# Crossbar transposes, 32x32 output tiles and a re-planned step order in a four-layer attention kernel

## The chip, the cores and the metric

The kernel runs on one core of one Trainium2 chip. The metric is the device time of one execution in microseconds (us). A profiled execution also has a span, from its first to its last instruction, which is a little shorter than its device time. Engines: TensorE (PE; PEld is its weight load), VectorE (DVE), ScalarE (ACT), GpSimd (POOL) and SyncE (SP), which issues almost all DMA transfers here.

## The reference, cut to what matters

Four layers work on one activation x of 2048 rows and 512 features, in the order A, B, A, B with the same weights for both A and both B. Each layer normalises x, computes an attention in 32 heads of 16 features, multiplies by an output matrix and adds the result to x.

```python
def _A_ref(x, wqkv, w_phi, wo):          # linear attention with learned features
    q, k, v = ...                        # x @ wqkv, heads of 16
    pq = einsum("bhsd,hdf->bhsf", q, w_phi)
    pk = einsum("bhsd,hdf->bhsf", k, w_phi)
    phi_q = concatenate([softmax(pq), softmax(-pq)])
    phi_k = concatenate([softmax(pk), softmax(-pk)])
    kv = einsum("bhsf,bhsd->bhfd", phi_k, v)     # sums over all 2048 rows
    z  = einsum("bhsf->bhf", phi_k)
    num = einsum("bhqf,bhfd->bhqd", phi_q, kv)
    den = einsum("bhqf,bhf->bhq", phi_q, z)[..., None] + 1e-6
    return (num / den) @ wo

def _B_ref(x, wqkv, wo):                 # window of 8 keys, 2 rows apart, looking back
    logits = einsum("bhsd,bhswd->bhsw", q, kg) * scale   # masked where the window leaves the sequence
    return einsum("bhsw,bhswd->bhsd", softmax(logits), vg) @ wo

x = x + _A_ref(layernorm(x), A...); x = x + _B_ref(layernorm(x), B...)   # twice
```

## The kernel before, in words

The 2048 rows are cut into four blocks (b = 0 to 3) of 512 rows, and each block into four tiles (t) of 128 rows. L = 0, 1 counts the pairs of layers. All products take bf16 inputs. Weight matrices, x and masks stay in SBUF; working tiles come from numbered slots of four pools ("big", "med", "t2" and the eight PSUM banks "ps").

The work is written as steps. Each `s_...` method of the class adds steps to threads, one thread for each stage and engine. The string `_ORDER` then says, step by step, which thread runs next, and so fixes the order of the instructions on TensorE, VectorE, ScalarE and on SyncE's queue: each engine works through its own list in that order and waits where an input or a buffer is not ready. `_CHOICE` has one digit for each flexible step (`flex`): a copy out of PSUM runs on VectorE (1) or ScalarE (0); a residual addition runs as one VectorE instruction (0, line 434) or as one more matmul with the identity on TensorE and a ScalarE copy (1, lines 424 and 431). `_SLOTS` names the buffer that each working tile gets. The setup (constants, masks, the first loads) stands in front of the steps and is not in `_ORDER`.

The stages:

- Fold (`s_fold`): the query and key weights of layer A are multiplied by `w_phi` once. The weights are transposed on TensorE (line 278), copied out, and multiplied by the block-diagonal `PHI` (line 289).
- Normalisation (`s_norm`): `ap` writes the normalised block xn (line 347). `pt` transposes it on TensorE, 16 transposes of 128x128 for a block (line 361), and `pe` copies the PSUM banks into xnT, two copies of 1024 columns for a block. A second way, `tr`, one transposing DMA for the whole block on SyncE's queue, stands in the code; `_OPT["tr_dma"]` names the blocks that take it, and is empty.
- Layer A, keys and values (`s_a1`): projections of keys (line 482) and values (line 494), exponentials of plus and minus the keys (line 488), softmax sums over f by three halving additions and a last one (`t8`, `t4`, `t2`, `t1`, lines 514 to 526), reciprocals through logarithm and exponential (`rr`), one product that normalises the exponentials (`mul`, line 534), and the key-value sums (`kv`, line 543): eight matmuls for each tile t, for the two signs and four groups of 128 columns, with 128 columns of features as weights and 129 moving columns (128 of values, and one of ones for z). They add up over all four blocks in three PSUM banks.
- Layer A, queries (`s_a2`): projections in transposed form (line 572), exponentials (line 580), softmax sums by small matmuls (line 588).
- `s_akv`: VectorE masks the finished sums into `ZM` (line 615) and into `R` (line 622), eight blocks of 128x128 of which the diagonal heads are kept. This needs the sums of all four blocks, so it separates the key side of a layer A from what follows.
- Layer A, denominators (`s_a3`): small matmuls with `ZM` (line 643), reciprocals, and the scaling of the query features, by broadcast matmuls for some blocks (lines 669 and 675) and by a DMA through DRAM for others (`Prho`).
- Layer A, output (`s_a4`): for each of four groups of heads two matmuls with a 128x128 block of `R` as weights and 512 moving columns (line 720), a copy into oT, then the output matrix (line 421), the residual and the statistics of the next normalisation (`s_out`).
- Layer B (`s_b1`, `s_b2`, `s_b3`): projections (line 742), a replication of the values along partitions by 16 DMAs for each block (`Vg`, line 794), the products with the window on VectorE (lines 823 and 883), sums of them by 32-column matmuls (lines 830 and 890), then the output matrix as in layer A. Block b needs the last rows of block b - 1.

Behind the last step a flag chooses whether a slower general path repeats the work; it is not taken for these inputs.

Of the kernel before, what the change touches and what calls it, by code (L numbers as in the profile page):

```python
# [19 lines left out]
H = 32  # L20
# [17 lines left out]
_OPT = {"rho_dma": ((0, 2), (0, 3), (1, 2), (1, 3)), "tr_dma": ()}  # L38
# [7 lines left out]
0 8l 0 4 4 1f 1 n 4 0 0 n 0 5 4 o 2 4 6 6 p n 2 n q u 3 u n n t 8 8 8 8 9 15 15 s 16 7 15 w 8 15 8 8 8 9i 17 v  # L46
a a a r u u y u b u 10 18 19 12 8 a i i z i i d d i 1g 1g 1d 1d c j i 13 13 1e 1e 1e x 12 13 13 d d k e i i i
1e 1d 1e 1e 12 12 k 1h l k 1d d 13 13 1i 11 d d d 2a d f f f f g 13 13 1a k m 1a 1a 1a 1g 1e 1e 1l 1l h 1z 20
2b 20 2c 1r 1z 20 1z 1z 20 1b 1r 1t 1l 2d 1l 1g 20 1k 2d 1s 20 20 20 1a 27 27 27 1o 1p 1o 11 11 14 1p 1p 1p 1r
1j 22 23 2c 2d 1o 1m 1p 22 1u 24 1p 27 1o 1l 1p 1p 2c 2c 2d 1w 22 22 1w 28 27 26 2d 2d 2d 25 1w 1w 1q 2b 2a 2b  # L50
1r 2a 2a 2d 1x 1c 1c 1c 1c 1n 2c 1n 1n 1n 2d 1w 1y 1y 1y 1v 1y 21 29 29 29 29 2b 2j 2j 2j 2j 2j 2j 31 2b 2b 2b
2b 2a 2b 2k 42 2l 2m 2l 2e 2e 43 2k 2l 2f 2l 2f 2f 2e 2l 2l 44 2f 43 2f 11 2e 2f 2f 2f 2k 2l 2l 2g 2h 2h 2e 2l
2f 5j 42 2g 2h 2l 2n 2n 2o 5k 43 43 2h 43 43 2n 5l 5k 5m 2p 2n 2g 2r 42 2g 43 32 43 43 43 2q 2s 2t 2s 2v 2s 45
45 ah 2h 2h 2w 45 2h 2h 46 47 2u 2u 2u 48 2s 2x 2u 2y 45 49 2u 2g 71 4a 2y 2y 2y 5m 4a 2y 4b 2s 2s 5m 2z 5k 5m
5k 2s 2s 4a 4e 4a 30 38 38 4c 2h 72 73 5n 5n 5n 4d 4c 11 4c 5o 3a 5p 72 33 33 4f 39 3d 5q 5n 4c 35 38 5r 5s 3b
34 4g 4c 3k 3d 4g 5s 5s 3e 2i 2i 5t 4g 4g 4a 4a 33 5w 4a 4g 4a 4h 3d 4i 5u 36 74 3f 74 74 3k 72 5v 5s 5u 5u 5x
5u 5y 5u 5y 74 38 4u 3c 4z 4u 4w 4p 4q 4p 4p 4r 72 3g 4k 4l 4k 4m 4k 51 4n 4v 75 75 77 76 4u 4x 3d 3h 3j 75 3i
4j 4u 4p 4y 5y 5y 5s 4t 5s 11 52 5y 3k 4k 78 50 51 4s 4o 51 75 79 5s 5s 60 7a 4j 7b 50 7c 7a 7d 7c 33 37 52 51
7a 7a 52 7f 5z 50 50 52 53 53 11 7e 7c 7c 3k 67 67 52 62 3l 7g 67 7c 7g 7a 7g 7g 7g 53 51 69 7a 7h 97 54 54 7a
7a 7i 3l 3l 3l 3m 3m 6c 6d 6c 6e 7p 7p 7q 68 3k 3l 6a 55 54 7k 7k 56 55 62 3m 7l 62 65 64 3j 54 7m 63 55 58 55  # L60
59 3j 3j 6c 3k 7u 6c 61 6f 6g 61 6i 7u 7p 67 3n 3o 6h 7w 6b 3n 3n 3n 3o 3q 6j 7p 7v 7s 6j 3o 3o 3s 7z 57 5a 5a
5d 5a 5b 3r 5c 6i 5a 5f 3p 3t 3t 3u 5c 3v 7k 5e 5c 6j 5c 5g 62 66 6j 5c 5g 3w 3v 3t 3t 3y 6k 6k 7r 6k 6k 6l 6l
5a 5g 5g 5a 6i 7u 5h 3x 5g 5a 5a 5i 81 7n 6k 6l 8x 81 8x 8y 7x 9t 9u 9t 9u 9u 9t 9t 3v 3v 6i 8u 7j 8x 9u 9u 9u
6j 6m 6n 6o 3z 3v 90 8x 7u 7y 8z 6m 6n 3z 3z 6p 8u 3z 7t 8v 3t 3t 3t 40 8u 91 8v 7k 7o 8v 8j 8j 9u 8v 8v 6m 6n
80 81 81 8k 3z 82 6q 82 8k 82 82 83 83 6m 3t 8m 82 83 6n 8u 8n 41 8v 6r 81 84 6s 6t 6s 9r 9s 6u 9s 6v 6u 9r 9s
6s 6s 8j 85 80 8k 8k 8k 8k 84 6w 6u 9u 8j 8k 80 80 84 8m 6x 9r 84 8k 86 6u 8m 8m 8v 6y 8v 8p 8o 92 6u 85 87 85
88 85 89 92 6y 6y 6y 92 6y 9r 9s 8a 8b 8a 9s 8d 6s 9s 9s 6s 6s 92 6z 9s 8a 8e 8a 9r 6s 8c 8c 9t 8c 8f 70 8c 9u
8r 95 95 95 93 8g 8r 8c 8g 8g 8g 8g 95 96 96 96 8r 8a 8a 8h 96 96 96 92 96 96 98 98 8a 8a 8i 9g 9h 98 9s 9g 8r
99 8s 9d 9g 98 9h 9h 9h 9h 9g 9d 9h 9h 9h 9d 9j 9k 8r 9j 9j 9b 9j 9l 9d 9v 9o 9e 9m 8t 8t 9o 8q 8w 8t 8t 9o 94
9o 94 94 94 9d 9f 9p 9o 9a 9f 9c 9f 9f 9q 9q 9q 9n 9q 9w 9z 9z 9w 9v 9w 9z 9z 9z 9z a0 9w a1 a2 a1 9v 9w 9w 9v  # L70
9w a0 bf 9w 9v 9w a1 a1 a1 a1 ct cu a0 cv a1 a1 a1 cu cw cw cw cw 9x 9y 9x 9x 9x 9y 9y 9y 9y a1 a3 a3 bg bh a4
a3 a3 a5 a6 a7 bg bf a8 a8 a9 9y 9y 9y aa bg bg bg bf bg bg bg bg bg a8 a8 ad 9x 9y bi bi bi ab ac bk bj aa aa
bl bi e8 bm aa ae aa bn bn bn e9 ea ae a8 ae ae ae br a8 af a8 a8 ag bo bn bq ao bp bp aj bs bp ao bp ak aj ao
cu bt bp ao cu bt cx cx cx al ap bt bt ar bt aq bn bn bu e9 cy bn bn bv cx eb eb eb eb aj am cz as aj bx d0 an
b0 b1 by b0 d1 c2 bx at b0 b0 bz b1 c3 d2 au c2 c2 c4 bx at at c5 c0 at cc ce ce av aw b1 b1 e9 ax ay bw d2 d2
d3 d2 d4 b2 b2 bx e9 c2 d5 d4 ce c7 b0 c1 b1 c6 ec d6 d4 b2 d7 d4 c8 ai az ce ec ec d8 d4 ed ee c7 c7 ca c9 b0
c7 cb ef d8 d2 cf ec eg d8 d8 cf az d2 d9 cf b3 cf cg cg bw d8 d2 d2 da eh cf cg ei eh az eh ek b3 b3 az dh eh
dh dr b3 dh dm el ej b4 dc b4 em cd ce cd cd ej ej ej en dn dc ch ej dj en eh en en eh eh en eh cd ch ch de eo
dm ep do dd dm dp di dt dt ci dm ci ck dh dk dq dl f6 ew db ds ds er es ex er ew ey ew et f1 f2 f1 b4 b7 er eu
ez f3 b5 f1 f4 b4 f1 f5 ch ew f0 er ev db eq f8 f8 b6 f9 f9 dc df du dc dg f8 f8 f9 f9 fa ci f7 fa dt dt f9 f7  # L80
f7 f7 b8 b9 fa cl du du du cj dv dv du ba b9 ds b9 b9 f8 fb fc fb fc dv dt ci be cm ds cn bb cn cn cr cn fe dw
fb fd fc ff fb dw fc fg fh fh fh cs fj dx dx dw dw dx fl dy fh cp fi fk dz co fn bc cq cq dx e1 fo e0 e2 e2 e2
e2 e3 bd bc fm fk e4 e5 e6 e7 fn e5
# [4 lines left out]
    "0110111000000011100001000000011001000000000000100011000000000111010010110000000000100000000000100000"  # L88
    "0010000000000000000000000110000100000000000000000000000001000001100000001000000010001001010000000000"
    "0000001111011100000000000000000000001111000000000000000000000000100000000011100000000000000000001110"  # L90
# [21 lines left out]
}


class _Fast:
# [152 lines left out]
    def s_fold(self, qk):  # L268
# [1335 lines left out]
```

## Time and profile before

| | |
|---|---|
| Time, median of 3 runs | 351.91 us (351.31 to 352.1) |
| Profiled execution, device time | 352.35 us |
| its span | 350.6 us |
| TensorE busy | 329.1 us (94% of the span) |
| VectorE busy | 316.4 us (90%) |
| ScalarE busy | 272.4 us (78%) |
| Mean granted TensorE clock | 0.997 |
| DMA, main queue | 30.09 MB, 40.6% of the 16 engines' span |

A group row of the profile names the source line, the engine, the operation, output and input tiles with their shapes, and the count; behind the first bar stand the busy time of the group in us and the mean duration of one instruction in ns, behind the second bar the idle time of the engine just before these instructions and what ended it. Matmuls overlap, so the mean duration of one is longer than busy time over count. A line can be that of a helper: lines 175 and 177 are all copies out of PSUM on VectorE and ScalarE. Rows of DMA issues give the count, the size of one and the median time from issue to landing.

### The profile page before, as it was taken

The page shows a single profiled execution, that of the slowest core. Times are in us where ns is not written, and L with a number is a line of the kernel's source. Part 1 is how long each engine was busy: PE and PEld are TensorE (multiplying, and loading weights), DVE is VectorE, ACT ScalarE, POOL GpSimd, SP SyncE. Part 2 cuts the span into 40 slices and gives each one's busy share as a digit, 9 for nine tenths or more (in the row PEclk, how much of TensorE's full clock was granted, in tenths as well). Part 3 has the DMA queues.
Part 4 walks back from the last instruction along what each step waited for, and adds up shares of the span by engine and source line. Part 5 has one row for each costly group of instructions (what it writes and reads, how often), then busy time and mean ns, then how long its engine had stood idle before and what let it go on. Part 6 is the DMA issues. An engine that isn't in the chain of part 4 may idle for free.

```text
span 350.6 us, 7264 instructions
## 1 busy us (share of the span) xinstructions
PE 329.1 (94%) x2829; PEld 166.5 (47%) x2854; DVE 316.4 (90%) x470; ACT 272.4 (78%) x613; POOL 4.2 (1%) x32
## 2 busy tenths in 40 slices
PE   0999999999999999999999999999999999998991
PEld 0855449545455454444434455754554544433330
DVE  7788894897989999999999999689999999999992
ACT  2679996777798797689999998588786897778460
POOL 3000000000000000000000000000000000000000
PEclk9999999999999999999999999999999999999998
DMA  7930000014040786680382000004032999439945
GB/s 226 351 100 1 2 0 2 4 35 109 20 111 22 178 201 125 110 139 1 67 148 35 2 0 2 3 6 125 1 69 74 158 161 159 83 69 163 154 112 169
DMA packets 17626, 30.65 MB, mean 87 GB/s; under 512 B 4272, under 2 KB 12464, under 8 KB 17584
## 3 DMA queue, kind: packets, MB, share of 16 engines
q1 hardware_dynamic: 17056, 30.09, 40.6%
q8 instruction: 24, 0.39, 0.6%
q14 instruction: 18, 0.15, 0.2%
q10 hardware_dynamic: 528, 0.02, 0.1%
HBM read 10.50 MB, written 2.36 MB: 37 GB/s over the span
## 4 chain that ended last, share of the span: by engine, by line
PE 74%; ACT 10%; DVE 7%; DMA 3%; issue 3%; SPq 2%; DVEq 0%; ACTq 0%
PE ps L742 23%; PE ps L421 11%; PE ps L494 7%; PE ps L482 6%; PE ps L361 4%; PE ps L543 4%; PE ps L572 4%; PE ps L830 3%; PE ps L720 3%; ACT Eq L580 3%; PE ps L890 3%; DVE pav L883 2%; SPq L794 2%; DVE Eq L675 2%; DMA wraw<-in_A_wqkv_dram 2%
## 5 line engine op out<-in xcount | busy, mean ns | idle before, releaser
L742 PE MATMUL ps<-xnT,WB 128*128 128x512 bf16 x384 | 90.0, 380 | 0.0
L883 DVE TENSOR_TENSOR pav<-PT,Vg 128x4096 bf16<-128x4096 bf16 x32 | 72.3, 2288 | 1.0 <-PE ps L424 0.2
L823 DVE TENSOR_TENSOR prod<-QT,K 128x4096 bf16<-128x4096 bf16 x32 | 72.0, 2287 | 0.2
L742 PEld LDWEIGHTS <-WB 128*128 128x128 bf16 x384 | 41.8, 114 | 42.7 <-issue 7.4
L421 PEld LDWEIGHTS <-oT 128*128 128x128 bf16 x256 | 23.7, 98 | 33.1 <-issue 3.5
L580 ACT ACTIVATE Eq<-ps 128x512 bf16<-128x512 f32 x64 | 34.7, 616 | 4.7 <-PE ps L572 4.7
L488 ACT ACTIVATE Ek<-ps 128x512 bf16<-128x512 f32 x64 | 34.7, 640 | 0.3
L177 ACT CAST oT<-ps 128x512 bf16<-128x512 f32 x52 | 29.9, 601 | 5.0 <-PE ps L890 3.2
L421 PE MATMUL ps<-WoB,oT 128*128 128x512 bf16 x123 | 31.6, 380 | 0.4
L421 PE MATMUL ps<-WoA,oT 128*128 128x512 bf16 x119 | 30.6, 379 | 1.2 <-DVE oT L175 0.4
L441 ACT ACTIVATE sqd<-x 128x512 bf16<-128x512 bf16 x48 | 30.0, 632 | 1.6 <-DVE x L434 1.6
L572 PE MATMUL ps<-xnT,WA 128*128 128x512 bf16 x128 | 31.0, 380 | 0.1
L482 PE MATMUL ps<-WA,xnT 128*128 128x512 bf16 x124 | 30.5, 379 | 0.3 <-issue 0.2
L494 PE MATMUL ps<-WA,xnT 128*128 128x512 bf16 x122 | 30.1, 379 | 0.3
L434 DVE SCALAR_TENSOR_TENSOR x<-ps,x 128x512 bf16<-128x512 f32 x43 | 28.3, 685 | 1.4 <-PE ps L421 1.0
L177 ACT COPY xnT<-ps 128x1024 bf16<-128x1024 bf16 x24 | 24.2, 1032 | 3.8 <-PE ps L361 3.7
L177 ACT CAST QT<-ps 128x512 bf16<-128x512 f32 x31 | 18.0, 598 | 8.1 <-PE ps L742 8.0
L675 DVE TENSOR_TENSOR Eq<-ps,Eq 128x512 bf16<-128x512 f32 x32 | 19.9, 683 | 1.1 <-PE ps L669 1.0
L177 ACT CAST V<-ps 128x512 bf16<-128x512 f32 x32 | 18.8, 600 | 2.5 <-PE ps L742 2.4
L177 ACT CAST K<-ps 128x512 bf16<-128x512 f32 x29 | 16.8, 595 | 4.8 <-PE ps L742 4.8
L431 ACT ACTIVATE x<-ps 128x512 bf16<-128x512 f32 x21 | 12.4, 598 | 10.0 <-PE ps L424 10.0
L361 PEld LDWEIGHTS <-xn 128*128 128x128 bf16 x256 | 16.8, 101 | 6.8 <-DVE xn L347 1.5
(117 smaller groups left out, 449.6 us busy)
## 6 DMA issues: line engine op xcount, KB each, us to landing
Vg<-V SPq DMA_DIRECT2D x128, 131.5 KB, 4.3
Prho<-rd SPq DMA_DIRECT2D x8, 512.0 KB, 4.6
out_dram<-x SPq DMA_DIRECT2D x8, 256.0 KB, 2.8
x<-in_A_x_dram SPq DMA_DIRECT2D x3, 512.0 KB, 8.6
WB<-in_B_wqkv_dram SPq DMA_DIRECT2D x3, 512.0 KB, 8.8
wraw<-in_A_wqkv_dram SPq DMA_DIRECT2D x2, 512.0 KB, 6.7
x<-in_A_x_dram SPq DMA_DIRECT2D x4, 128.0 KB, 2.6
WA<-in_A_wqkv_dram SPq DMA_DIRECT2D x1, 512.0 KB, 4.3
```

Of the source, the lines that this page charges most:

```text
L177: self.nc.scalar.copy(out=out, in_=in_)
L361: nc.tensor.transpose(U["pt", t // 2][:, (t % 2 * NB + c) * P:(t % 2 * NB + c + 1) * P], self.xn[key, b][:, t, c * P:(c + 1) * P], self.id ...
L421: nc.tensor.matmul(y[:], lhsT=oT[:, c, t * P:(t + 1) * P], rhs=Wo()[:, c, :], start=(c == 0), stop=(c == NB - 1 and not onpe))
L441: nc.scalar.activation(out=sqd[:], in_=xb[:, t, :], func=ACT.Square, accum_out=T["ss"][:, t:t + 1])
L482: nc.tensor.matmul(pk[:], lhsT=xnT[:, t, k, :], rhs=self.WA[:, k, D:2 * D], start=(k == 0), stop=(k == NB - 1))
L488: nc.scalar.activation(out=T["E"][:, t, s, :], in_=T["k", t][:], func=ACT.Exp, scale=1.0 - 2.0 * s)
L494: nc.tensor.matmul(pv[:], lhsT=xnT[:, t, k, :], rhs=self.WA[:, k, 2 * D:3 * D], start=(k == 0), stop=(k == NB - 1))
L572: nc.tensor.matmul(pq[:], lhsT=self.WA[:, k, hb * P:(hb + 1) * P], rhs=xnT[:, :, k, :], start=(k == 0), stop=(k == NB - 1))
L580: nc.scalar.activation(out=self.Eq[L, b][s][:, :, hb, :], in_=T[hb][:].rearrange("p (t i) -> p t i", t=4), func=ACT.Exp, scale=1.0 - 2.0 * s)
L742: nc.tensor.matmul(pp[:], lhsT=self.WB[:, k, i * D + c:(i + 1) * D:NB], rhs=xnT[:, :, k, :], start=(k == 0), stop=(k == NB - 1))
L823: nc.vector.tensor_tensor(out=pr[:], in0=QT[:, c:c + 1, :].to_broadcast([P, NW, TB]), in1=win, op=ALU.mult)
L883: nc.vector.tensor_tensor(out=pv[:], in0=PT[:].unsqueeze(1).to_broadcast([P, NB, 2, TB]), in1=vw, op=ALU.mult)
```

## The change

- `_OPT["tr_dma"]` now names every block of every layer but block 0 of the first layer A: 15 of 16 blocks are transposed by one DMA each. In block 0 of the first layer the normalisation goes in parts of one, one and two tiles.
- `fold_dma`: the query weights are transposed by four DMAs straight from DRAM.
- The features are now ordered by head and then f, so PHI, the masks and the softmax sums have f innermost: the halving additions work on rows of 8, 4, 2 and 1, and `rr` writes each reciprocal twice, for rows of 2 in `mul`.
- `kv`: for each tile t 16 matmuls with the values of one pair of heads and a column of ones as weights (33 columns) and 64 moving columns, at column tiles 0 and 64, in one PSUM bank instead of three.
- `s_akv`: the sums are copied to SBUF (two flexible copies), transposed by four TensorE transposes and masked by three VectorE products; `R` shrinks to eight blocks of 32 columns.
- `s_a4`: the output product is one step of 32 matmuls on 32x32 tiles in four PSUM banks. The rows of `WoA` are loaded in the new order, by four DMAs.
- Loads and masks become steps in `_ORDER`, and the key weights come in two halves; 14 matmuls on zeros (`warm`) stand at the start of TensorE's list.
- `_ORDER`, `_CHOICE` and `_SLOTS` are new throughout. Of the 64 residual additions 36 instead of 21 go over TensorE and ScalarE.

```diff
-_OPT = {"rho_dma": ((0, 2), (0, 3), (1, 2), (1, 3)), "tr_dma": ()}
+_OPT = {
+    "rho_dma": ((0, 2), (0, 3), (1, 2), (1, 3)),
+    "tr_dma": tuple((k, b) for k in ("A0", "B0", "A1", "B1") for b in range(4) if (k, b) != ("A0", 0)),
+    "fold_dma": (0,),
+    "warm": 14,
+}
...
+        def warm():
+            if not hasattr(self, "warm_ps"):
+                self.warm_ps = self.ps()
+            nc.tensor.matmul(self.warm_ps[:], lhsT=self.kvT[:, 0:P], rhs=self.kvT[:], start=True, stop=True)
...
+        def lraw(qk, h):
+            if qk not in self.wraw:
+                self.wraw[qk] = self.med([NB, D], "wraw")
+            c = qk * D + h * 256
+            nc.sync.dma_start(out=self.wraw[qk][:, :, h * 256:(h + 1) * 256], in_=wav[:, :, c:c + 256])
...
+        def trd(hb):
+            tile()
+            c = qk * D + hb * P
+            nc.sync.dma_start_transpose(out=T["wT"][:, hb, :], in_=self.A_wqkv[:, c:c + P])
...
         def view():
-            return T["E"][:].rearrange("p t s (hb f hl) -> p (t s hb) f hl", hb=NB, hl=8)
+            return T["E"][:].rearrange("p t s (g f) -> p (t s g) f", f=DH)
 
         def t8():
-            T["s8"] = self.med([G, 8, 8], "s8")
-            nc.vector.tensor_tensor(out=T["s8"][:], in0=view()[:, :, 0:8, :], in1=view()[:, :, 8:16, :], op=ALU.add)
+            T["s8"] = self.med([G, 8], "s8")
+            nc.vector.tensor_tensor(out=T["s8"][:], in0=view()[:, :, 0:8], in1=view()[:, :, 8:16], op=ALU.add)
...
         def mul():
-            nc.vector.tensor_tensor(out=view(), in0=view(), in1=T["r"][:].unsqueeze(2).to_broadcast([P, G, 16, 8]),
+            ev = view().rearrange("p g (a two) -> p g a two", two=2)
+            nc.vector.tensor_tensor(out=ev, in0=ev, in1=T["r"][:].unsqueeze(2).to_broadcast([P, G, 8, 2]),
                                     op=ALU.mult)
 
         def kv(t):
             if L not in self.kvp:
-                self.kvp[L] = [self.ps() for _ in range(3)]
-            for s in range(2):
-                for hb in range(NB):
-                    i = s * NB + hb
-                    nc.tensor.matmul(self.region(L, i), lhsT=T["E"][:, t, s, hb * P:(hb + 1) * P],
-                                     rhs=T["va"][:, t, hb, :],
-                                     start=(b == 0 and t == 0 and i % 3 == 0),
-                                     stop=(b == 3 and t == 3), skip_group_check=True)
+                self.kvp[L] = self.ps()
+            K = self.kvp[L]
+            for r in range(4):
+                for h2 in range(2):
+                    for c in range(2):
+                        q = (2 * c + h2) * 4 + r
+                        a = K[64 * c:64 * c + H + 1, h2 * 256 + r * H:h2 * 256 + r * H + 1]
+                        out = bass.AP(a.tensor, a.offset, [list(a.ap[0]), [P, 2], [1, H]])
+                        nc.tensor.matmul(out, lhsT=T["va"][:, t, q, :], rhs=T["E"][:, t, :, q * H:(q + 1) * H],
+                                         start=(b == 0 and t == 0 and r == 0 and h2 == 0),
+                                         stop=(b == 3 and t == 3), tile_position=(0, 64 * c), skip_group_check=True)
...
+        def ev(c, dve):
+            self.copy(dve, self.kvT[64 * c:64 * c + H + 1, :], self.kvp[L][64 * c:64 * c + H + 1, :])
+
+        def tr():
+            T["t"] = pt = self.ps(BF16)
+            for g in range(4):
+                nc.tensor.transpose(pt[:, g * P:(g + 1) * P], self.kvT[:, g * P:(g + 1) * P], self.ident[:])
...
-        def mo(hb):
-            T[hb] = po = self.ps()
+        def mo():
+            for r in range(4):
+                T[r] = self.ps()
             for s in range(2):
-                nc.tensor.matmul(po[:], lhsT=self.R[:, s * NB + hb, :], rhs=self.Eq[L, b][s][:, :, hb, :],
-                                 start=(s == 0), stop=(s == 1))
+                for hb in range(NB):
+                    for r in range(4):
+                        nc.tensor.matmul(T[r][32 * hb:32 * hb + 32, :],
+                                         lhsT=self.R[32 * r:32 * r + 32, self.reg(s, hb), :],
+                                         rhs=self.Eq[L, b][s][32 * r:32 * r + 32, :, hb, :],
+                                         start=(s == 0), stop=(s == 1), tile_position=(32 * r, 32 * hb))
```

The transposing DMA itself was in the code already:

```python
        def tr():
            xnT = self.med([4, NB, P], "xnT")
            nc.sync.dma_start_transpose(out=xnT[:].rearrange("k t c p -> k (t c) p"),
                                        in_=self.xn[key, b][:].rearrange("p t d -> p (t d)"))
```

350 lines of the change are left out of this document (196 added, 154 removed).

## The prediction

> **What bounds the kernel now.** I read first the busy time of each engine over the whole span and its forty slices, then the chain that ended last, then a table of eight stretches, whose borders I put where the work changes.
>
> ```profile
> span 350.6 us, 7264 instructions
> PE 329.1 (94%) x2829; PEld 166.5 (47%) x2854; DVE 316.4 (90%) x470; ACT 272.4 (78%) x613; POOL 4.2 (1%) x32
> ...
> DMA  7930000014040786680382000004032999439945
> ...
> PE 74%; ACT 10%; DVE 7%; DMA 3%; issue 3%; SPq 2%; DVEq 0%; ACTq 0%
> ```
>
> TensorE is the first limit (74% of the chain), but VectorE is 13 us behind it: taking work from TensorE alone buys little. The stretches show which one limits where (columns: span, then busy us and instructions of PE, PEld, DVE, ACT, POOL, then granted clock, DMA share, GB/s).
>
> ```profile
> 0.00:15.40 15.40, 6.43 (x66) 6.25 (x68) 11.98 (x40) 5.96 (x10) 3.05 (x25) 1.00 0.90 280
> 15.40:64.00 48.60, 48.44 (x480) 28.72 (x483) 38.96 (x69) 40.45 (x87) 0.63 (x5) 1.00 0.12 35
> 64.00:100.00 36.00, 34.86 (x355) 17.50 (x356) 32.76 (x71) 29.32 (x66) 0.00 (x0) 1.00 0.21 53
> 100.00:160.00 60.00, 59.70 (x414) 27.85 (x416) 57.12 (x70) 48.99 (x118) 0.34 (x2) 1.00 0.59 122
> 160.00:240.00 80.00, 78.38 (x787) 40.92 (x794) 73.69 (x105) 70.30 (x161) 0.00 (x0) 1.00 0.18 36
> 240.00:275.00 35.00, 34.84 (x262) 17.28 (x264) 34.43 (x55) 26.77 (x64) 0.15 (x1) 1.00 0.29 67
> 275.00:330.00 55.00, 53.70 (x386) 23.60 (x388) 53.83 (x47) 42.55 (x98) 0.00 (x0) 1.00 0.84 133
> 330.00:350.60 20.60, 12.75 (x91) 4.44 (x89) 13.60 (x19) 8.07 (x15) 0.00 (x0) 0.95 0.57 143
> ```
>
> First layer A (15.4 to 64) is TensorE alone: 48.4 of 48.6 us, with VectorE and ScalarE at 39 and 40. From 64 to 160 and from 240 to 330 TensorE and VectorE are both full; 160 to 240 is TensorE's again. The stretch 275 to 330 also has the DMA engines at 0.84. The profiled execution took 352.35 us, 1.75 more than its span and 0.44 above the median of 351.91; my sums are against the span, and I add 1.75.
>
> **TensorE, part by part.** "Mean ns" includes the overlapped latency, so I price one instruction as busy time over count.
>
> ```profile
> L361 PE MATMUL ps<-ident,xn 128*128 128x128 bf16 x256 | 19.8, 225 | 0.0
> L278 PE MATMUL ps<-ident,wraw 128*128 128x128 bf16 x32 | 3.4, 290 | 8.9 <-DMA wraw<-in_A_wqkv_dram 8.9
> L543 PE MATMUL ps<-vaug,Ek 128*128 128x129 bf16 x256 | 15.6, 221 | 0.0
> L720 PE MATMUL ps<-Eq,R 128*128 128x512 bf16 x64 | 16.1, 379 | 0.0
> L588 PE MATMUL ps<-Eq,indS 128*32 128x128 bf16 x256 | 5.5, 220 | 0.1
> L643 PE MATMUL ps<-Eq,ZM 128*32 128x128 bf16 x256 | 4.8, 219 | 0.0
> L669 PE MATMUL ps<-rho,indB 32*128 32x128 bf16 x128 | 3.6, 217 | 0.9 <-DVE rho L662 0.8
> L890 PE MATMUL ps<-pav,indAV 128*32 128x512 bf16 x256 | 18.0, 383 | 0.8 <-DVE pav L883 0.6
> L421 PE MATMUL ps<-WoB,oT 128*128 128x512 bf16 x123 | 31.6, 380 | 0.4
> ```
>
> Transposes of xn: 256 become 16, so 240 x 19.8/256 = 18.6 us go. Of the 32 fold transposes 16 go (the query half, now four transposing loads): 16 x 3.4/32 = 1.7.
>
> Key-value sums: 256 matmuls of 129 columns (15.6 us) become 512 of 64 columns, two side by side. Nothing shows this shape. The four-wide small matmuls start every 4.8/256 = 18.8 ns (L643) or 21.5 ns (L588) although a full-width 128-column one takes 77 (L361). I take 21.5, an issue rate rather than array time, since 64 columns two-wide are as much array time as 128 four-wide: 512 x 21.5 = 11.0, a gain of 4.6. Ends: 18.8 ns gives a gain of 6.0; no overlap at twice the rate (43 ns) gives 22, a loss of 6.4.
>
> Output product: 64 matmuls of 512 columns (16.1) become 256 on 32x32 tiles. Four-wide 512 columns cost 18.0/256 = 70 ns; were sixteen to run together, 70/4 = 17.6 ns. Row tiles with one bank each (L669) start every 28 ns. I take 28, the row nearest in kind: 7.2 us, a gain of 8.9; ends 4.5 us (gain 11.6) and 18.0 us (loss 1.9). [...]
>
> Added: the residual goes onto TensorE 36 times in place of 21 (by the choice string), 15 x 31.6/123 = 3.9; eight transposes of the key-value sums, 0.6. The 14 warming matmuls cost 14 x 0.26 = 3.6 us (L421's rate), under the 15.40 - 6.43 = 9.0 us in which TensorE is idle in the first stretch; without that cover they cost 3.6. Sum: -18.6 -1.7 -4.6 -8.9 +3.9 +0.6 = -29.3; TensorE 329 -> 300.
>
> **VectorE and ScalarE.**
>
> ```profile
> L434 DVE SCALAR_TENSOR_TENSOR x<-ps,x 128x512 bf16<-128x512 f32 x43 | 28.3, 685 | 1.4 <-PE ps L421 1.0
> L434 DVE DVE_READ_ACCUMULATOR x<-ps,x 128x1 f32 x38 | 3.2, 83 | 0.0
> L175 DVE COPY xnT<-ps 128x1024 bf16<-128x1024 bf16 x8 | 5.5, 686 | 1.2 <-PE ps L361 0.9
> L175 DVE CAST oT<-ps 128x512 bf16<-128x512 f32 x12 | 8.0, 686 | 0.2 <-PE ps L890 0.2
> L514 DVE TENSOR_TENSOR s<-Ek 128x2048 bf16<-128x2048 bf16 x8 | 9.8, 1221 | 1.1 <-ACT Ek L488 1.0
> L534 DVE TENSOR_TENSOR Ek<-Ek,rk 128x4096 bf16<-128x4096 bf16 x8 | 18.3, 2287 | 1.5 <-ACT rk L531 1.5
> L622 DVE TENSOR_TENSOR R<-ps,maskR 128x384 bf16<-128x384 f32 (+1 forms) x6 | 2.7, 504 | 0.0
> L615 DVE TENSOR_TENSOR ZM<-ps,maskR 128x24 bf16<-128x24 f32 (+1 forms) x6 | 0.9, 180 | 5.8 <-PE ps L543 5.8
> L177 ACT COPY xnT<-ps 128x1024 bf16<-128x1024 bf16 x24 | 24.2, 1032 | 3.8 <-PE ps L361 3.7
> L431 ACT ACTIVATE x<-ps 128x512 bf16<-128x512 f32 x21 | 12.4, 598 | 10.0 <-PE ps L424 10.0
> L431 ACT ACTIVATION_READ_ACCUMULATOR x<-ps 128x1 f32 x10 | 2.0, 198 | 0.0
> L531 ACT ACTIVATE rk<-s 128x256 bf16<-128x256 f32 x8 | 3.3, 416 | 2.0 <-DVE Ek L534 1.8
> ```
>
> The 64 residual additions go from 43 on VectorE to 28 (by layer A, B, A, B the moved ones are 4, 6, 6, -1, so the last layer gets none): 15 x 0.66 = 9.9, and 16 accumulator reads x 0.08 = 1.3. Evacuations of xnT: 8 become 2, 6 x 0.69 = 4.1. oT: 12 become 7, 5 x 0.67 = 3.3. K, QT and the fold net -1 x 0.69. The masking of the sums (2.7 + 0.9 for L622 and L615) becomes per layer one 256-element product and two tiny ones, 1.6 in all at L615's 0.18 and twice that for the product, less 2.0; one copy of the sums per layer adds 1.4. Sum: -9.9 -1.3 -4.1 -3.3 -0.7 -2.0 +1.4 = -19.9; VectorE 316 -> 297. The halving sums and the normalising product (L514, L534) keep their element counts, but their innermost rows fall from 64 and 8 elements to 8, 4, 2 and 1: I take that as free. The other end is half the rate, as of the float source in L434 (512 elements in 0.66 us against 2048 in 1.22): 9.8 + 18.3 = 28 us more, rival (b).
>
> ScalarE: 24 copies of 1.01 become one (-23.2); 15 residuals x 0.59 (+8.9) and 16 reads x 0.20 (+3.2); five oT copies (+3.0) and two of the sums (+1.2), each 0.6 like L431; K and QT -0.6; the reciprocal writes 512 elements instead of 256 in eight places, 0.2 each (+1.7). Sum -5.8; 272 -> 267.
>
> **The wait that comes in.** A block's transpose is now one 512 KB transfer on SyncE's queue, and nothing in the trace transposes by DMA.
>
> ```profile
> Prho<-rd SPq DMA_DIRECT2D x8, 512.0 KB, 4.6
> WB<-in_B_wqkv_dram SPq DMA_DIRECT2D x3, 512.0 KB, 8.8
> Vg<-V SPq DMA_DIRECT2D x128, 131.5 KB, 4.3
> ```
>
> Plain 512 KB transfers land after 4.6 to 8.8 us. I take 5.5, near the lower row since that one too runs while the cores compute and not in the load burst, plus something for the reordering. Today the way from the last xn to a usable xnT is 16 x 0.077 + 1.0 = 2.2 us, so each block comes 3.3 us later. What covers it: in the new step order TensorE work of 3 to 5.4 us (a step of four projections counted as 0.9 us, a little under L421's 4 x 0.26) stands between a block's last normalisation and its first projection in 11 of 15 places, more than 7 in two, under 1 in two (blocks 2 and 3 of the first layer B, where VectorE has 5 to 8 us of its own). At 5.5 us the exposed rest is about 1 us in most places; I charge 2 us at the two layer entries from A to B. The four query-fold transposes are 128 KB each and have the key projections of block 0 as cover. Behind each transpose SyncE's queue holds the next loads: WoA, WB and then Vg; the first two are needed late, the Vg issue is delayed by up to one transpose (its own wait for V is what is late next).
>
> The key-value barrier grows: copy 0.6, transposes 0.3, two masks 0.4 in place of 0.5, plus hand-overs: +2 us in each layer A, covered in part by one small TensorE step; I charge it whole.
>
> [...]
>
> **The sum, by stretch.** First stretch: the first weights come as 256 KB ahead of three of the x tiles, and TensorE waits for weights until 8.9 us:
>
> ```profile
> PE ps L278 <- DMA wraw<-in_A_wqkv_dram: 8.9, 1, 8.9
> ```
>
> about -2: VectorE's constants, part of its 11.98 us there, move partly into first layer A, where it has 48.6 - 39.0 = 9.6 to spare. First layer A: TensorE 48.4 loses 48 transposes (3.7) and half of the key-value gain (2.3), +2 for the barrier: -4; ScalarE's 40.5 is not reached. 64 to 100: TensorE -6, VectorE -5, but +2 for the late transpose: -3. 100 to 160: VectorE at 57.1 sets it, -4 (its residuals and copies); TensorE falls as much. 160 to 240: TensorE -6 (64 transposes, sums), +2 for the barrier: -4; ScalarE at 70.3 allows no more than 9. 240 to 330: VectorE 88.3 loses 4 to 5, mostly residuals of the second layer A: -5. Last stretch: a drain of products, copies and stores, 0. Total -2 -4 -3 -4 -4 -5 = -22: span 328.6, with 1.75 about **330**.
>
> **Rivals.**
> (a) The crossbar is late: slower. At 8.8 us a block (the slow row) the excess over 4.5 us of cover is 4.3; it is paid wherever TensorE and VectorE both run dry, at least at the 12 block entries behind the first layer: up to 52 us, less the 22 won: 382 at most; with half of it hidden, 356. It decides from about 22/12 + 4.5 = 6.3 us if none is hidden, 8.2 us if half is. For it: sharing a queue with Vg, whose landing row is 4.3 for a quarter of the bytes. Against: 11 places of cover. [...]
> (b) The short rows cost: VectorE runs them at half rate, +14 us in each layer A. First layer A: 39 - 3 + 14 = 50 in place of 44.6, +5; 160 to 240: 73.7 - 4 + 14 = 84 in place of 76, +8: 343. VectorE 90% busy speaks for it; that L514 and L534 already take rows of 64 and 8 at the same rate per element, against.
> (c) The DMA engines limit the last layer: at 0.84 for 55 us, its Vg transfers need 46 us whatever the engines do, and two transposes (1 MB at 133 GB/s, 8 us) fall among them. The stretch from 240 on then gains nothing and loses 3 to 5: 339.
> (d) The small tiles don't overlap: TensorE gets back 11.0 + 10.8 = 22 us, mostly in layer A stretches where it limits: 345.
> (e) Everything is hidden: the charges of 2 us for two barriers and the late transpose fall away (6), and the 6 of VectorE's 19.9 us that I left outside its critical stretches count there too: 330 - 6 - 6 = 318.
>
> **How the numbers follow.** Forecast 0.34 (324 to 336), (a) 0.15, (b) 0.17, (c) 0.14, (d) 0.07, (e) 0.13. 317 to 353 leaves out the upper part of (a), little of (e), and is a range for 8 in 10. 0.2% is 0.7 us, about what this measurement can tell from no change. Faster: all but (a) and its neighbours, 0.82; same 0.03; slower 0.15.
>
> **What would show it.** Right: TensorE near 300 busy, VectorE near 297, ScalarE near 267; the transposes' landing at 5 to 6.5 us; key-value matmuls together near 11 us and the output product near 7; waits of TensorE on xnT of a few us in sum. Wrong: landings over 8 us, or TensorE's longest waits all on xnT; DMA share at 9 tenths from 240 on with VectorE idle before its pav products; the largest halving sum above 1.22 us.

## The result, and the profile after

The changed kernel takes 339.15 us (median of four runs, 337.56 to 342.65) against 352.0 for the kernel before: ratio 0.962, 95% interval 0.957 to 0.967. It is 12.9 us faster; the forecast was 22 (330 us). The ratio leaves out the slowest of the four runs (342.65 us, mean granted clock 0.977), which the median holds; the median of the other three is 338.22, so the differences from 339.15 told below are uncertain by about 1 us. The profiled execution has a span of 338.4 us (340.08 us of device time). Its page, the lines that answer to those of before:

```profile
span 338.4 us, 7769 instructions
PE 310.9 (92%) x3083; PEld 144.6 (43%) x3083; DVE 298.6 (88%) x425; ACT 266.6 (79%) x629; POOL 5.9 (2%) x32
...
PEclk9999999999999999999999999999599999999999
...
PE 52%; DVE 21%; DMA 11%; ACT 7%; issue 4%; SPq 2%; DVEq 0%; ACTq 0%
PE ps L845 20%; PE ps L500 12%; DMA xnT<-xn 4%; DMA Prho<-rd 4%; PE ps L993 4%; PE ps L655 4%; DVE Ek L613 4%; PE ps L933 3%; DVE s L590 2%; DMA x<-in_A_x_dram 2%; DVE stat L470 2%; PE ps L570 2%; DVE xn L423 2%; DVE pav L986 2%; PE ps L558 2%
```

VectorE and ScalarE do what was forecast (298.6 and 266.6; forecast 297 and 267). The span does not follow: VectorE's busy time fell by 17.8 us, the span by 12.2, so its idle time grew. The chain that ended last has 11% of DMA where it had 3%: 4% are the transposes, 2% the first loads of x, and 4% the broadcast of rho (`Prho<-rd`), the factors that scale the query features and that four blocks write to DRAM (`rd`) and read back onto all partitions. One slice of the clock shows a 5.

To see where the time went, I cut each execution at five events: the first mask of each layer A (`ZM`), the first projection of each layer B, and the last window product of the first layer B. Lengths in us; the last three rows are experiments told below.

| | first layer A, to its mask | mask to B | first B, into second A | to second mask | mask to B | last B, end | span |
|---|---|---|---|---|---|---|---|
| before | 61.4 | 25.2 | 107.0 | 31.0 | 24.5 | 101.6 | 350.6 |
| after | 53.9 | 24.2 | 102.5 | 30.8 | **28.2** | 98.8 | 338.4 |
| rho free (e7) | 53.5 | 23.5 | 102.4 | 31.1 | 24.7 | 96.1 | 331.3 |
| old read order (e9) | 53.7 | 23.3 | 100.0 | 30.7 | 24.7 | 96.6 | 329.0 |
| two copies (e10) | 53.8 | 23.3 | 100.4 | 30.5 | 25.9 | 96.5 | 330.4 |

The second way from mask to layer B got 3.7 us longer. The two stretches, of before and after (span; busy us of PE, PEld, DVE, ACT, POOL; granted clock, DMA share, GB/s):

```profile
224.50:249.00 24.50, 23.58 (x353) 11.97 (x353) 22.03 (x52) 18.54 (x45) 0.00 (x0) 1.00 0.18 48
```
```profile
211.40:239.60 28.20, 22.64 (x446) 10.66 (x447) 21.25 (x46) 20.37 (x54) 0.00 (x0) 0.98 0.32 60
236.00:238.00 2.00, 0.10 (x16) 0.10 (x27) 1.68 (x3) 0.00 (x0) 0.00 (x0) 1.00 0.87 196
240.00:244.00 4.00, 4.00 (x11) 1.47 (x10) 2.69 (x8) 3.36 (x10) 0.00 (x0) 0.50 0.22 60
```

TensorE and VectorE are busy for less and the stretch is longer. From 236 to 238 TensorE does almost nothing (0.10 us), and from 240 to 244 it runs at half clock. SyncE's queue in that stretch (start, duration of the issue), then VectorE's two products with rho:

```profile
220.77 0.58 SPq L781 DMA_DIRECT2D rd<-rho  x1
223.42 0.68 SPq L788 DMA_DIRECT2D Prho<-rd  x1
224.14 0.57 SPq L781 DMA_DIRECT2D rd<-rho  x1
229.66 0.63 SPq L788 DMA_DIRECT2D Prho<-rd  x1
231.17 4.87 SPq L429 DMA_TRANSPOSE xnT<-xn  x1
```
```profile
231.61 1.22 DVE L792 TENSOR_TENSOR Eq<-Eq,Prho 128x2048 bf16<-128x2048 bf16 x1
236.28 1.22 DVE L792 TENSOR_TENSOR Eq<-Eq,Prho 128x2048 bf16<-128x2048 bf16 x1 [3.46 <-DMA Prho<-rd]
```

The second write (32 KB) is issued behind the first read (512 KB), and its own read only 5.52 us later; that read is in use 6.62 us after its issue. VectorE waits 3.46 us for it and TensorE behind VectorE (1.98 us). I took this stall for a matter of the queue's order; it lies in one line of the change.

### The profile page after: what moved, and what is told of

Read it like the earlier page. It is cut to its first block, busy times and chain, and to the rows that moved or that the text cites. A ratio compares the mean times of both kernels' runs of the same rounds, so it can differ in the third digit from the quotient of the medians.

```text
span 338.4 us, 7769 instructions
## 1 busy us (share of the span) xinstructions
PE 310.9 (92%) x3083; PEld 144.6 (43%) x3083; DVE 298.6 (88%) x425; ACT 266.6 (79%) x629; POOL 5.9 (2%) x32
## 4 chain that ended last, share of the span: by engine, by line
PE 52%; DVE 21%; DMA 11%; ACT 7%; issue 4%; SPq 2%; DVEq 0%; ACTq 0%
PE ps L845 20%; PE ps L500 12%; DMA xnT<-xn 4%; DMA Prho<-rd 4%; PE ps L993 4%; PE ps L655 4%; DVE Ek L613 4%; PE ps L933 3%; DVE s L590 2%; DMA x<-in_A_x_dram 2%; DVE stat L470 2%; PE ps L570 2%; DVE xn L423 2%; DVE pav L986 2%; PE ps L558 2%
## 5 line engine op out<-in xcount | busy, mean ns | idle before, releaser
L845 PE MATMUL ps<-xnT,WB 128*128 128x512 bf16 x384 | 90.0, 385 | 4.2 <-DMA xnT<-xn 2.0
L845 PEld LDWEIGHTS <-WB 128*128 128x128 bf16 x384 | 42.7, 115 | 47.8 <-issue 8.2
L180 ACT CAST oT<-ps 128x512 bf16<-128x512 f32 x57 | 31.6, 597 | 10.5 <-PE ps L993 7.6
L500 PE MATMUL ps<-WoA,oT 128*128 128x512 bf16 x128 | 32.8, 390 | 0.5 <-DVE oT L178 0.2
L564 ACT ACTIVATE Ek<-ps 128x512 bf16<-128x512 f32 x64 | 32.9, 617 | 0.0
L510 ACT ACTIVATE x<-ps 128x512 bf16<-128x512 f32 x36 | 21.2, 600 | 7.5 <-PE ps L503 7.2
L180 ACT CAST K<-ps 128x512 bf16<-128x512 f32 x30 | 17.7, 596 | 6.2 <-PE ps L845 6.2
L513 DVE SCALAR_TENSOR_TENSOR x<-ps,x 128x512 bf16<-128x512 f32 x28 | 18.8, 686 | 2.1 <-PE ps L500 2.0
L993 PE MATMUL ps<-pav,indAV 128*32 128x512 bf16 x256 | 17.0, 382 | 3.3 <-DVE pav L986 3.0
L180 ACT CAST QT<-ps 128x512 bf16<-128x512 f32 x29 | 17.0, 589 | 3.2 <-PE ps L845 3.2
L570 PEld LDWEIGHTS <-xnT 128*128 128x128 bf16 x128 | 12.2, 98 | 15.9 <-DVE xn L423 1.0
```

The source lines that it names most:

```text
L180: self.nc.scalar.copy(out=out, in_=in_)
L500: nc.tensor.matmul(y[:], lhsT=oT[:, c, t * P:(t + 1) * P], rhs=Wo()[:, c, :], start=(c == 0), stop=(c == NB - 1 and not onpe))
L564: nc.scalar.activation(out=T["E"][:, t, s, :], in_=T["k", t][:], func=ACT.Exp, scale=1.0 - 2.0 * s)
L570: nc.tensor.matmul(pv[:], lhsT=xnT[:, t, k, :], rhs=self.WA[:, k, 2 * D:3 * D], start=(k == 0), stop=(k == NB - 1))
L845: nc.tensor.matmul(pp[:], lhsT=self.WB[:, k, i * D + c:(i + 1) * D:NB], rhs=xnT[:, :, k, :], start=(k == 0), stop=(k == NB - 1))
L993: nc.tensor.matmul(po[32 * c:32 * c + 32, :], lhsT=self.indAV[:], rhs=T["p", q][:, c, hf, :], start=(hf == 0), stop=(hf == 1), tile_positi ...
```

## The experiments

First theory (T1): the missing 9 us are waits at the entries from layer A to layer B, where rho's round trip through DRAM and the transposes share SyncE's queue and the DMA engines. Rival (T2): VectorE and TensorE are simply full. Four runs.

**e1, rho's writes and reads early.** In the code, beside the order string, in which the second read moves up behind the first, and a few buffer numbers:

```diff
-        for s in range(2):
-            if dma:
-                add(st, "SP", wr, s)
-                add(st, "SP", rdb, s)
+        if dma:
+            for s in range(2):
+                add(st, "SP", wr, s)
+        for s in range(2):
+            if dma:
+                add(st, "SP", rdb, s)
```

> The changed kernel with the order of SyncE's queue altered and nothing else: for each of the four blocks whose rho goes through DRAM, both writes are issued before the first read, and the second read stands right behind the first, ahead of the transpose that stood between them in blocks 2 and 3 of the first layer. Theory T1 (the missing 9 us are waits at the entries from layer A to layer B, where rho's round trip and the transposes share SyncE's queue and the DMA engines): in the changed kernel the second write of block 2 of the second layer A was issued at 224.14 behind a 512 KB read, its own read only at 229.66, and VectorE waited 3.46 us for it, after which TensorE's clock was 0.50 for some 6 us (about 3 us lost). With the writes first the second read is issued near 225 and lands near 231: entry from the second layer A to layer B 28.2 -> 24 to 25 us, no slice with half clock, and 1 to 2 us at the first layer's entry: 333 to 335 against 339. Rival T2 (VectorE and TensorE are simply full, the waits are hidden by other work somewhere): within 1 us of 339.

Measured: 343.65 us (340.65 to 344.85), 4.5 slower than the changed kernel. Neither theory has this. SyncE's queue at the first entry, and the stretch that follows:

```profile
72.01 6.57 SPq L427 DMA_TRANSPOSE xnT<-xn  x1
83.42 1.19 SPq L779 DMA_DIRECT2D rd<-rho  x2
85.37 1.39 SPq L786 DMA_DIRECT2D Prho<-rd  x2
86.86 9.25 SPq L427 DMA_TRANSPOSE xnT<-xn  x1
```
```profile
77.00:80.00 3.00, 0.00 (x0) 0.00 (x0) 1.31 (x3) 2.97 (x10) 0.00 (x0) 1.00 0.87 176
81.00:85.00 4.00, 4.00 (x12) 1.53 (x11) 2.61 (x8) 0.98 (x3) 0.00 (x0) 0.57 0.04 8
```

The transposes now queue behind 1 MB of reads (6.57 and 9.25 us of SyncE each, against 3.14 and 5.22 in the changed kernel), TensorE stands still for three microseconds and then runs at little over half clock. The second entry got shorter (26.9 us against 28.2), the first one longer (27.3 against 24.2). So the two do compete, and in this order rho's gain was the transposes' loss: moving rho ahead is no remedy.

**e2, the fifteen transposes back on TensorE**, with their copies on ScalarE (`tr_dma` empty; `pt` and `pe` steps a little behind the normalisation, in free PSUM banks).

> The changed kernel with all fifteen block transposes back on TensorE (240 more matmuls of 128 columns and 30 copies, all on ScalarE); the folding weights still come by transposing loads, everything else as changed. Prices from the kernel before: TensorE +18.6 us, ScalarE +30 us. T1 (the crossbar's gain on TensorE is largely eaten by waits for it, and the queue and the DMA engines are slowed for rho too): +3 to +7, 342 to 346, with the A-to-B entries no longer than in the kernel before. T2 (the engines' sums set the time): +12 to +16, 351 to 355, since TensorE is the limit in layers A and ScalarE's 267 becomes 297.

Measured: 364.46 us (363.44 to 366.78), +25, more than either theory. TensorE 329.6 busy, ScalarE 294.1. The stretch to the second mask, where it lost 6 us against after's 30.8:

```profile
196.50:233.50 37.00, 32.56 (x441) 16.96 (x439) 27.43 (x46) 32.61 (x71) 0.00 (x0) 0.99 0.01 2
```

ScalarE's 32.6 us, which were 27.5 in the changed kernel, are now as many as TensorE's. The step order was not planned anew for it, so +25 is the price of TensorE's transposes in this order, not what the transposing DMA alone is worth.

**e3, the output product at full size.**

```diff
-            for s in range(2):
-                for hb in range(NB):
-                    for r in range(4):
-                        nc.tensor.matmul(T[r][32 * hb:32 * hb + 32, :], lhsT=self.R[32 * r:32 * r + 32, ...], ...)
+            for hb in range(NB):
+                for s in range(2):
+                    nc.tensor.matmul(T[hb][:], lhsT=self.R[:, 4 * s:4 * s + 4, :]..., rhs=self.Eq[L, b][s][:, :, hb, :], ...)
```

> The changed kernel with the layer A output product as 64 matmuls of 128x128 weights and 512 columns again (as many and as wide as before the change); the weights are columns of the same masked sums but not the right ones, so its output is not the reference's. TensorE +9.6 us (16.1 against 6.5), 1.2 us in each of eight blocks, all in or near the entries from layer A to layer B. T1 (TensorE waits there for rho and the transposes): +2 to +5, since part of it fills waits. T2: +8 to +10.

Measured: 339.08 us, the median of six runs: five from 336.8 to 340.85 and one of 1822.5 us (why it came was not examined; without it the median is 338.96). Its product is busy 15.8 us in place of 6.5, and the time is that of the changed kernel: nine microseconds of TensorE work cost nothing. They filled waits: VectorE waits 2.0 us for rho in place of 5.1. And in the profiled execution the clock does not halve before the drain, where that of the changed kernel is half for 6.8 us; so TensorE's busy time is only 3.2 us longer (314.1). The clock is not the whole of it: the fastest runs of the two kernels, at mean clocks of 0.998 and 0.999, took 337.56 (changed) and 336.8 us (e3).

**e4, sixteen residual additions back on VectorE** (sixteen digits of `_CHOICE`).

> The changed kernel with sixteen of its 36 residual additions back on VectorE (the fifteen net ones that the change moved, and one more): VectorE +16 x 0.66 + 16 x 0.08 = +11.8, TensorE -16 x 0.26 = -4.2 or, by the changed kernel's row for them (13.6 us for 36), up to -6, ScalarE -16 x 0.8 = -13. Ten of the sixteen stand at the A-to-B entries, six in the first layer B. T2 (VectorE full in layer B and at the entries): +6 to +9. T1 (waits set the entries): 0 to +4, the first layer B alone giving 2 to 4.

Measured: 355.38 us (354.43 to 358.62), +16.2, twice what T2 asks for. VectorE's busy time grew by 10.0 (308.6); the rest I put down, untested, to an order made for other engines: TensorE waits 4.0 us for one residual at 136, and the clock is half in three places (0.982 in the mean).

So T2 fell for TensorE (e3) and T1's remedy made it worse. Three causes were left: transposes that come late (A), rho's round trip (B), or the engines' own work and hand-overs (C). The next runs take each away.

**e5 and e6, projections that need no transpose**: they read the normalised block itself (e5); in e6 the transposes are issued all the same and nobody waits.

```diff
-            self.xnT[key, b] = xnT
+            self.xnT[key, b] = _Plain(self.xn[key, b])      # the block itself, seen as [p, t, c, i]
```

> The changed kernel without the fifteen block transposes: the projections read the normalised block itself, untransposed, so the output is not the reference's, but every projection has the same size and waits only for VectorE's normalisation. It prices all that the transposes cost by coming late and by loading SyncE's queue and the DMA engines. Theory A (the gain that is missing was lost to transposes that come late, TensorE waiting on xnT 6.1 us in sum and what follows from it): 330 to 333, 6 to 9 under the changed kernel's 339. Theory B (it was lost to rho's round trip through DRAM): 336 to 338. Theory C (VectorE's and ScalarE's own work and hand-overs set the time; sixteen residuals on VectorE had cost 16 us, 9 us more TensorE work nothing): 338 to 339.

> As the run before, but the fifteen transposes are still issued at their places in SyncE's queue and land in tiles that nobody reads: no projection waits for them, their load on the queue and on the DMA engines stays. Theory A with waits as the price: as the run before, within 1 us. If the load on the DMA engines and on the queue is the price (rho and Vg later by it): near the changed kernel, 336 to 339, with rho's waits as there (3.5 us at the second entry).

Measured: 338.63 (336.85 to 339.6) and 341.03 (340.7 to 341.94). Without the fifteen transposes the time is the same: late transposes alone are not the missing 9 us, and theory A fell. That e6 is 2.4 us above e5 I put down to the transposes' load on queue and DMA engines (its tiles also lie in other buffers); why it is above the changed kernel too stays open. In e5 the wait of VectorE for rho is still there (us in total, times, longest):

```profile
DVE Eq L801 <- DMA Prho<-rd: 5.4, 3, 4.3
```

**e7, rho's round trip left out.**

```diff
-            nc.vector.tensor_tensor(out=ev[:], in0=ev[:], in1=T["P", s][:], op=ALU.mult)
+            nc.vector.tensor_tensor(out=ev[:], in0=ev[:], in1=self.WoA[:]..., op=ALU.mult)   # wr, rdb: no steps
```

> The changed kernel without rho's round trip in the four blocks that have it: writes and reads are left out and VectorE multiplies by a constant tile of the same size (layer A's output weights), so the output is not the reference's; the transposes stay. Theory B: 333 to 335, the second A-to-B entry 28.2 -> 24.5 and no half clock behind it. Theory A: 337 to 338, only the 3.5 us wait of VectorE and part of the half clock at the second entry going. Theory C: within 1 us.

Measured: 332.81 us (331.7 to 333.17), 6.3 less, the second entry 24.7. Theory B holds: most of the loss was rho's.

**e8, rho's transfers issued by GpSimd** (`nc.gpsimd.dma_start` in `wr` and `rdb`).

> The changed kernel with rho's eight writes and eight reads issued by GpSimd instead of SyncE, all else alike: GpSimd is idle (5.9 us busy), so rho no longer stands behind a transpose in SyncE's queue nor a transpose behind rho's reads, while the bytes on the DMA engines are the same. If the shared queue is the price at the entries (the first experiment moved rho ahead and only made the transposes late, by 4 us each): 334 to 336. If the DMA engines are: 338 to 340. Slower than 340 if GpSimd's issues themselves take longer than SyncE's 0.6 us.

Measured: 349.61 us (346.21 to 351.08). This other queue doesn't help: TensorE waits longer for the transposes (first fence, its waits; 2.0 and 4.1 us in sum in the changed kernel), and the reads land 9.9 us after their issue (second, the DMA issues).

```profile
PE ps L845 <- DMA xnT<-xn: 8.9, 3, 4.8
PEld L845 <- DMA xnT<-xn: 7.1, 3, 5.2
```
```profile
Prho<-rd POOLq DMA_DIRECT2D x8, 512.0 KB, 9.9
```

Why should rho cost more than before, where the same four blocks took it? The DMA share while a read alone is under way answers. Before, then after:

```profile
238.00:239.50 1.50, 1.49 (x22) 0.62 (x21) 1.45 (x3) 1.17 (x4) 0.00 (x0) 1.00 1.00 275
```
```profile
225.00:227.50 2.50, 2.50 (x28) 1.03 (x26) 2.50 (x6) 2.50 (x10) 0.00 (x0) 1.00 0.54 159
```

The same 512 KB have a DMA share of 1.00 before (275 GB/s) and of 0.54 after (159 GB/s). The change has one line on this, which the new order of the features needs:

```diff
-            src = bass.AP(a.tensor, a.offset, [[0, 16], [2 * 16 * P, 8], [1, 16 * P]])
+            src = bass.AP(a.tensor, a.offset, [[2 * 16 * P, 8], [0, 16], [1, 16 * P]])
```

The outermost step of the source went from sixteen entries to eight, and the share while it reads to about half. Nothing had shown at this point that the one follows from the other. Theory D, then: this line. Rival E: the round trip is as long as it was and only its cover has shrunk.

**e9, that line alone put back.**

> The changed kernel with one line put back as it was before the change: the source of rho's 512 KB read steps over the eight rows inside and over the sixteen repeats outside, as in the kernel before (there one read landed 4.6 us after its issue; in the changed kernel the last one at the second A-to-B entry took 6.6 us, and the read between had held back the small write behind it for 5.5). The rows then land in the wrong partitions, so the output is not the reference's. Theory D (the changed order of the source makes the read slower, and this is what lengthened the entries): landing back to about 4.6 us, VectorE's wait of 3.5 us at the second entry gone, no half clock behind it, 333 to 335.5. Rival E (the round trip is as long as it was, only the work that covered it has shrunk): landing stays near 6.6, 338 to 340.

Measured: 330.74 us (330.37 to 333.76), ratio to the kernel before 0.940 (0.936 to 0.944): 8.4 us from one line (7.8 by the two ratios), and less than the 333 to 335.5 that theory D asked for. Share and rate while it reads, the product with rho in VectorE's timeline, the reads' landing, and the page's clock line:

```profile
221.30:222.80 1.50, 1.50 (x23) 0.64 (x21) 1.50 (x3) 1.50 (x5) 0.00 (x0) 1.00 0.99 279
```
```profile
227.86 2.42 DVE L792 TENSOR_TENSOR Eq<-Eq,Prho 128x2048 bf16<-128x2048 bf16 x2
```
```profile
DMA to landing us min/median/max: 4.5/4.7/5.7
```
```profile
PEclk9999999999999999999999999999999999999998
```

VectorE runs its two products back to back with no wait, and no slice of the clock is low before the drain. Rival E fell. That e7, with no round trip at all, is 2.1 us slower than this has its place in the table: 102.4 us against 100.0 in the third stretch, where TensorE stood still for 2.4 us from 138.6 in e7 and then had half clock for 3.4 us. So part of the 8.4 us, too, is clock and not reading: the 6.8 us at half clock in the changed kernel's execution are worth up to 3.4.

**e10, sixteen rows with the right values**: every row of rho is written twice.

```diff
-            dst = bass.AP(a.tensor, a.offset, [[P, 16], [2 * 16 * P, 8], [1, P]])
-            nc.sync.dma_start(out=dst, in_=T["rho"][:, s, :])
+            dst = bass.AP(a.tensor, a.offset, [[P, 16], [2 * 16 * P, 8], [16 * P, 2], [1, P]])
+            nc.sync.dma_start(out=dst, in_=T["rho"][:, s, :].unsqueeze(1).to_broadcast([P, 2, P]))
...
+            src = bass.AP(a.tensor, a.offset, [[16 * P, 16], [0, 8], [1, 16 * P]])
```

> The changed kernel with every row of rho written twice to DRAM (64 KB a write in place of 32), so that the read steps over sixteen rows outside and eight repeats inside; the values are the right ones. If the read is slow because its outermost step has only eight entries to be spread over the DMA engines, it is fast again and this is 334 to 336, a version faster than both. If it is slow because neighbouring partitions read the same row one after the other, little changes: 338 to 340. Rival E: 338 to 341, the write being larger.

Measured: 332.15 us (330.41 to 334.76), ratio 0.943 (0.939 to 0.947) where the changed kernel has 0.962 (0.957 to 0.967). This version is faster than both kernels, and a little faster than forecast. Neighbouring partitions still read one row here, eight in a row, so that is not what made the read slow. What the fast reads have in common is sixteen outer entries (share 1.00 before, 0.99 in e9, 0.92 here); the slow one has eight (0.54). How a transfer is spread over the DMA engines no trace shows. Share while it reads, and landing:

```profile
221.70:223.20 1.50, 1.50 (x22) 0.64 (x21) 1.50 (x3) 1.50 (x6) 0.00 (x0) 1.00 0.92 265
```
```profile
DMA to landing us min/median/max: 4.3/4.8/5.6
```

**e11, the kernel before with that line alone.**

> The kernel before with only that line of the change: rho's read in the new order of its source (rows in the wrong partitions, so the output is not the reference's). Theory D: the read's landing goes from 4.6 to 6 to 7 us; the time by 0 to +3 (352 to 355), since the second read at the second entry landed near 246 there and was first used at 250.7, about 5 us of slack. Rival E: landing 4.6 as it was, time within 0.7 of 352.

Measured: 356.22 us (355.38 to 357.45), +4.2 (ratio 1.010, 1.007 to 1.014). I had looked for slack at the second entry, and there it did hold (24.5 as before); the cost came behind the first entry (111.7 in place of 107.0), where VectorE waited 4.7 us for one read (idle us and times before its products with rho) and TensorE stopped behind it:

```profile
  DMA Prho<-rd: 4.7, 1
```
```profile
89.00:92.00 3.00, 0.00 (x0) 0.00 (x0) 1.11 (x1) 0.00 (x0) 0.00 (x0) 1.00 0.20 45
92.00:97.00 5.00, 4.83 (x15) 1.90 (x15) 4.97 (x14) 3.55 (x11) 0.00 (x0) 0.66 0.05 10
```

**e12, e3's full-size product on top of e10.**

> The kernel with two copies of rho's rows (332.15 us) and, on top, the layer A output product as 64 full-size matmuls again (wrong weights of the same size, so the output is not the reference's): TensorE +9.3 us by the rows of the run that did this on the changed kernel, where it cost nothing (339.08 against 339.15). If it cost nothing there because TensorE was waiting for rho at the entries, it costs now, where that wait is 1.2 us: +3 to +6, 335 to 338. If VectorE's work sets the entries whatever rho does: within 1.5 of 332.

Measured: 336.43 us (334.85 to 339.37), +4.3. The 9.3 us of TensorE that were free while rho was late now cost almost half their length. The small tiles pay, but the changed kernel could not show it.

## Why the prediction was right in its direction and 9 us off

The forecast had the direction, and 339.15 lies in its range of 317 to 353, but none of the rivals is what happened. The step that failed is one that isn't there: the sum prices every moved transpose and matmul, and takes rho's broadcast as it was. The row that I quoted for it (`Prho<-rd`, 512 KB, 4.6) was even my reference for the transposes' landing; that its source is read in another order after the change was one line of the full diff, left out of the cut shown above, and I gave it no price. The runs put it at 8.4 us on the changed kernel (e9) and 4.2 on the kernel before (e11). Two slips stand beside it: I charged 2 us at both entries from A to B, but the sum has the charge only at the first (64 to 100), so the entry that grew by 3.7 us had none; and the new masks are 1.4 us by the rows I took, not 1.6. The forecast's stretches against the executions, from the table above (its borders 64 and 240 are 61.4 and 249 there):

| | forecast | after | with the old read order (e9) |
|---|---|---|---|
| start and first layer A | -2 - 4 = -6 | -7.4 | -7.7 |
| from there to the second layer B | -3 - 4 - 4 = -11 | **-2.0** | -8.9 |
| second layer B and drain | -5 + 0 = -5 | -2.8 | -5.1 |
| sum | -22 | -12.2 | -21.7 |

The failed terms are those of 64 to 100, 100 to 160 and 160 to 240, and a part of the -5: rho late, and half clock behind the stop. With the one line back the sum is met, partly by luck: its middle is still 2 us short and its start 2 us better.

Of the rivals, (a), the late crossbar (the transposing DMA), fell with e5; its landing is 4.8 us where I took 5.5. (b), dear short rows, fell by the rows below: 1218 and 2287 ns against 1221 and 2287. (c), the DMA engines as the limit of the last layer, gave 339, the measured number, but by coincidence: e9 gains the whole 5 us there with the transposes in place. (d) fell: the small tiles overlap (one lasts 383 ns in the mean, 256 of them are busy 6.5 us, 25 ns each). (e), everything hidden (318), fell too: even e9 takes 330.74. My terms against the rows, groups first and then the transposes' issues:

```profile
L627 PE MATMUL ps<-Ek,vaug 128*33 128x64 bf16 x512 | 8.6, 193 | 0.8 <-issue 0.6
L821 PE MATMUL ps<-Eq,R 32*32 32x512 bf16 x256 | 6.5, 383 | 4.8 <-DVE Eq L772 2.0 <-DVE s L748 2.0 <-DVE Eq L792 0.7
L503 PE MATMUL ps<-x,ident 128*128 128x512 bf16 x36 | 13.6, 379 | 0.0
L590 DVE TENSOR_TENSOR s<-Ek 128x2048 bf16<-128x2048 bf16 x8 | 9.7, 1218 | 0.0
L613 DVE TENSOR_TENSOR Ek<-Ek,rk 128x4096 bf16<-128x4096 bf16 x8 | 18.3, 2287 | 0.3 <-ACT rk L608 0.3
```
```profile
xnT<-xn SPq DMA_TRANSPOSE x15, 4.8
```

- Key-value sums: 8.6 us (8.6/512 = 16.8 ns each) against 11.0.
- Output product: 6.5 (25 ns each) against 7.2.
- Residual: 13.6/36 = 0.38 us each, where I counted 0.26, L421's rate before: 15 more are 5.7 by this row, not 3.9.
- TensorE in sum: 310.9 less 5.6 for the warming matmuls is 305; forecast 300 without them. The busy time also holds what the half clock stretches: from 239.57, at a clock of 0.50, eight projections (L845) took 3.57 us, 0.45 each, against 90.0/384 = 0.23 over the whole span.
- "VectorE sets it", my reading of 64 to 160 and 240 to 330, is borne out in kind: 9.3 us of TensorE were free (e3), 10 us of VectorE cost 16 (e4). It holds only while rho is late: with rho on time TensorE's 9.3 us cost 4.3 (e12), so the two engines share the limit. In number VectorE's part was not isolated, since e4 upsets the order too.

What the transposes' waits cost where rho isn't late was not tried; e5 prices them only with the slow read in place. Nor was e2's order planned anew.

## What to carry to other kernels

Price every line of a diff that reorders a DMA's access pattern: here the outermost dimension of a read went from sixteen entries to eight and its DMA share, while it ran alone, from 1.00 to 0.54. That share is the thing to look at. Where a stretch has less work and more time, leave out one suspect at a time with the work unchanged: it told rho from the transposes in two runs, where moving either only moved the wait. And an engine that waits hides what it would gain, so test a saving again once the wait is gone (e3 against e12).

## What the runs showed of the hardware that I had not expected

- A block's transpose takes no time of a computing engine, but it holds the queue: its issue kept SyncE for 4.87 us in the row shown (1.3 to 5.7 over the fifteen), against 0.6 for a plain transfer.
- The changed kernel's reads of rho issued by GpSimd landed 9.9 us after their issue (e8); the one shown from SyncE was in use after 6.62.
- A short stop of TensorE can be paid twice, first as the stop and then as half clock. In e1 it did nothing from 77 to 80 and had a mean clock of 0.57 from 81 to 85; in e11 nothing from 89 to 92 and 0.66 from 92 to 97; in the changed kernel it was busy for 0.10 us from 236 to 238 and had 0.50 from 240 to 244. The stops were 3.9 us long in all in e1, 3.3 in e11 and 2.0 in the changed kernel. The four runs of the changed kernel stand in the order of their mean granted clock (337.56 us at 0.998, 338.22 at 0.989, 340.08 at 0.988, 342.65 at 0.977). But the length of a stop alone does not decide: in e8 TensorE stood still for 3.2 us, from 78 to 80 altogether, and kept its clock. What decides stays open.

```profile
78.00:80.00 2.00, 0.00 (x0) 0.00 (x0) 1.15 (x2) 1.72 (x6) 0.00 (x0) 1.00 0.86 193
81.00:86.00 5.00, 5.00 (x54) 2.37 (x52) 4.25 (x12) 2.82 (x9) 1.77 (x4) 1.00 0.06 16
```
